# A Fourier filter woven into a feed-forward block: the forward transform over s by three real products per complex one

## The chip, the cores and the metric

The kernel runs on one core of a Trainium2 chip. The metric is the device time of one execution in microseconds (us); the time before is the median of three runs. A profile is one further execution, recorded by the hardware profiler.

## The reference, cut to what matters

```python
def reference(x, w_r, w_i, _, w1, w2):            # x 1 x 2048 x 1024, F = 3584
    xn = layernorm(x)
    X = rfft2(xn, axes=(-2, -1))                  # 2048 x 513, complex
    s = irfft2(X * (w_r + 1j * w_i), (2048, 1024), axes=(-2, -1))
    g = silu(silu(xn @ w1) @ w2)
    return x + s * g
```

One branch is a two-dimensional Fourier filter, the other a feed-forward block; both start from the same normalised rows and meet in the last line. The axis of 2048 rows is called s, the axis of 1024 columns d.

## The kernel before

**The feed-forward block** is the bulk of the work of PE, the matmul engine (TensorE). `mm1` (line 456, tile `pa`) multiplies the rows by w1 in groups of 24 matmuls of 128x512; `mm2` (lines 539 to 541, tile `pb`) multiplies by w2 in seven products of a Strassen-like scheme, in half-groups of 21 matmuls. Between the two the hidden rows go to DRAM as sums and differences (`hd_sum`, `hd_one`, `hd_dif`) and come back as `ht`. Weights for w2 come in 256 KB pieces (`jr`, line 412), and are converted by ACT and DVE (ScalarE and VectorE, tile `w`, lines 251 and 254).

**The filter branch** is cut into generators that are woven between these groups. `ln_gen` normalises; `fd_gen` (lines 798 to 893) is the forward transform over d, four blocks c of 512 rows; `f_gen` (from line 924) is the forward transform over s with the filter and the first part of the inverse; `edge_gen` treats the last column; `i_gen` is the inverse, for the four c in the order 1, 3, 0, 2, with tile `iu` (lines 1204 and 1212) and tile `id` (line 1294), and a butterfly behind each `id` (lines 1305 to 1340).

At its end `fd_gen` makes for each c four results j: `radix4` writes `Ro` (real part in columns 0 to 127, imaginary in 128 to 255 of each of four rows q). `high_r` (ACT) and `low_r` (DVE, line 865) split it into a high and a low f16 half, `Rs`, and a deferred SP instruction stores `Rs` in the DRAM tile `vd{j}` (line 866). When all is stored, `close` (through `switch`) frees the pool of this stage, and `open_f` opens the next one, in the same memory.

`f_gen` works through 16 blocks u = 4q + j. `load_v` brings `vq{u}` (512 KB, two buffers), `load_w` the two filter pieces `wq` (256 KB each, four buffers), `load_k`, issued by ACT, the constants `kq` for each q. `mat(u)` computes the complex product with the constants k = (-sin, cos, sin) on PE, tile `fx`. For each of four c and each of three pairings of high and low halves it issues one matmul of 256 columns with cos (both parts at once) and two of 128 columns with the sines: 36 matmuls, lines 954 to 956. `fx` fills one of the two PSUM buffers with tag `ft`, which `fa`, `fx`, `iu` and `id` share. `copy(u)` (ACT, line 975) copies half of `fx` to SBUF, and two instructions of DVE of 512 elements (`xb` and `xd`, lines 1004 and 1005) add and subtract the halves. Then DVE multiplies by the filter and transforms back, `T`, `yb`, `yd`, `Z`, `zq`.

**What sets the order.** Everything is written out by hand in one program order; each engine takes its instructions in that order and waits on semaphores. After every group of `pa` or half-group of `pb` the function `work` lets the next step of a generator run, as long as a model of DVE's time is not over a model of PE's by more than `LEAD` = 1 us. `meter` keeps both models: an instruction of DVE adds a fixed and a per-element part.

```python
    COST = {"DVE": ("dve", 0.12, 1.05e-3), "PE": ("pe", 0.0, 0.4215e-3)}
...
            clock["dve"] = max(clock["dve"], clock["pe"] - 1.0)
            for _ in range(3):
                if clock["dve"] > clock["pe"] + LEAD or hold[0] or slot(bg) == PAUSE:
                    break
```

`defer(n, fn)` issues fn n such ticks later. Nearly all DMAs are issued by SP (SyncE), strictly in order. SP's DMAs use eight semaphores in turn, `DMAHW0` to `DMAHW7`, and a DMA waits until the one before it on the same semaphore has landed.

Of the kernel before, what the change touches and what calls it, by code (L numbers as in the profile page):

```python
# [43 lines left out]
def make_constants():  # L44
# [16 lines left out]
    k = np.stack([-np.sin(th), np.cos(th), np.sin(th)], 3)  # L61
# [66 lines left out]
def spectral_ffn(ctx, tc, x, w_r, w_i, w1, w2, ca, kc, ci, tw, pm, out):  # L128
# [19 lines left out]
    vd = [dp.tile([128, 4, 4, 2, 256], F16, name=f"vd{j}") for j in range(4)]  # L148
    zd = [dp.tile([128, 4, 2, 1024], F16, name=f"zd{c}") for c in range(4)]
# [62 lines left out]
    COST = {"DVE": ("dve", 0.12, 1.05e-3), "PE": ("pe", 0.0, 0.4215e-3)}  # L212
# [563 lines left out]
    psa, l0 = {}, {}  # L776

# [17 lines left out]
    def fd_gen(c):  # L795
# [3 lines left out]
        def bfly(p):  # L799
            t0 = l0.pop((c, p))  # L800
            tt, stt = nc.vector.tensor_tensor, nc.vector.scalar_tensor_tensor
# [56 lines left out]
        o, sp = {}, {}  # L858

        def high_r(j):  # L860
            sp[j] = ap.tile([128, 4, 2, 256], F16, name=f"Rs{c}_{j}", tag="Rs", bufs=2)
            nc.scalar.activation(sp[j][:, :, 0], o[j], AF.Copy, scale=2.0**-21)
# [55 lines left out]
    def open_f():  # L918
# [3 lines left out]
        B["k"], B["v"], B["w"], B["z"] = {}, {}, {}, {}  # L922

    def f_gen():
# [12 lines left out]

        def load_w(u):
# [8 lines left out]
        def mat(u):  # L947
            q = u // 4
            ps = pt.tile([128, 4, 2, 128], F32, name=f"fx{u}", tag="ft")
            v, k = B["v"].pop(u), B["k"][q]  # L950
            for c in range(4):
                o = ps[:, c].rearrange("m r k -> m (r k)")
                for n, (kh, vh) in enumerate(((0, 0), (0, 1), (1, 0))):
                    nc.tensor.matmul(o, k[:, c, kh, 1], v[:, c, vh], start=(n == 0), stop=False)  # L954
                    nc.tensor.matmul(ps[:, c, 0], k[:, c, kh, 2], v[:, c, vh, 128:256], start=False, stop=False)  # L955
                    nc.tensor.matmul(ps[:, c, 1], k[:, c, kh, 0], v[:, c, vh, 0:128], start=False, stop=(n == 2))
            psx[u] = ps
# [3 lines left out]
        load_v(0)  # L961
        load_w(0)
# [33 lines left out]
        for u in range(16):  # L996
# [3 lines left out]
            ps, cpy = psx.pop(u), cps.pop(u)  # L1000
            pv = ps.rearrange("m c r k -> m c (r k)")
            b = bp.tile([128, 2, 2, 128], F32, name=f"xb{u}", tag="xb", bufs=1)
            d = bp.tile([128, 2, 2, 128], F32, name=f"xd{u}", tag="xd", bufs=1)
            tt(b.rearrange("m c r k -> m c (r k)"), pv[:, 0:2], cpy, op=OP.add)
            tt(d.rearrange("m c r k -> m c (r k)"), pv[:, 0:2], cpy, op=OP.subtract)
# [619 lines left out]
```

## Time and profile before

| | us |
|---|---|
| median of three runs | 1235.48 |
| the runs | 1234.14 to 1237.49 |
| the profiled execution | 1235.84 |
| its span | 1234.1 |
| PE busy | 1220.7 (99%) |
| DVE busy | 999.0 (81%) |
| ACT busy | 467.6 (38%) |
| POOL (GpSimd) busy | 117.3 (10%) |

The span runs from the first to the last recorded instruction; the profiled execution's own time has in addition what lies around it. In rows of a timeline the first number is the start in us from the start of the span, the second the duration; `x3` says that the row holds three instructions; a bracket at the end tells how long the engine was idle before it, and what it waited for. Matmuls are pipelined: they start more closely than their durations say. The granted clock of PE was at its full value in every part of the profile.

### The profile page before, as it was taken

Reading aid. Unit: us, or ns where it says so; the run is one execution under the profiler, and the core shown is the slowest. Engines: PE = TensorE matmul, PEld = TensorE weight load, DVE = VectorE, ACT = ScalarE, POOL = GpSimd, SP = SyncE. Lnnn points to the kernel's source line nnn. Section 1 sums busy time; section 2 is a strip of 40 time slices with the busy share of each in tenths; the row PEclk is TensorE's granted clock in tenths of the full one; section 3 lists DMA queues with packets and bytes.
Section 4 is the critical chain, followed back from the end, with each engine's and each line's share of the span. In section 5 each row is a group of like instructions: output and inputs, shape, how many; then the busy total and the mean of one; then the engine's idle time right before and its main releaser. Section 6 shows DMA issues by size and latency. Waiting matters only on the chain.

```text
span 1234.1 us, 19097 instructions
## 1 busy us (share of the span) xinstructions
PE 1220.7 (99%) x7033; PEld 625.2 (51%) x7033; DVE 999.0 (81%) x1970; ACT 467.6 (38%) x614; POOL 117.3 (10%) x245
## 2 busy tenths in 40 slices
PE   8999999999999999999999999999999999999998
PEld 5545445444544454445545555554455555555545
DVE  7687988899798898896969899985186678798886
ACT  4865344333554565444433222122032222243212
POOL 2330000001000000010001121114111111000000
PEclk9999999999999999999999999999999999999999
DMA  7487476655758898759898999997989999998576
GB/s 253 134 172 187 135 224 201 185 152 161 223 172 237 276 283 242 217 177 279 207 283 224 283 259 198 276 256 246 293 207 278 286 289 331 315 332 325 200 261 260
DMA packets 271102, 293.67 MB, mean 238 GB/s; under 512 B 40096, under 2 KB 198816, under 8 KB 270624
## 3 DMA queue, kind: packets, MB, share of 16 engines
q1 hardware_dynamic: 250992, 233.66, 65.7%
q10 hardware_dynamic: 15984, 51.45, 12.0%
q0 software_dynamic: 4032, 7.34, 3.5%
q8 instruction: 55, 0.90, 0.3%
q14 instruction: 39, 0.32, 0.1%
HBM read 185.95 MB, written 102.25 MB: 234 GB/s over the span
## 4 chain that ended last, share of the span: by engine, by line
PE 75%; DVE 11%; DMA 9%; issue 2%; ACT 1%; SPq 0%; POOL 0%; DVEq 0%; ACTq 0%; POOLq 0%
PE pa L456 45%; PE pb L539 8%; PE pb L541 8%; PE pb L540 8%; DVE Z L1055 2%; DMA wq<-in_A_w_i_dram 2%; DMA sd<-s 2%; PE id L1294 2%; DMA zd<-zq 1%; DMA ht<-hd_sum_d 1%; DVE T L1020 1%; DVE w L254 1%; PE iu L1204 1%; ACT xp L709 1%; PE iu L1212 1%
## 5 line engine op out<-in xcount | busy, mean ns | idle before, releaser
L456 PE MATMUL pa<-xnT,w 128*128 128x512 f16 x2688 | 585.2, 379 | 1.1 <-ACT w L251 0.7
L456 PEld LDWEIGHTS <-w 128*128 128x128 f16 x2688 | 262.2, 98 | 311.6 <-DVE w L254 1.3
L539 PE MATMUL pb<-w,ht 128*128 128x512 f16 (+2 forms) x812 | 300.4, 372 | 0.0
L540 PE MATMUL pb<-w,ht 128*128 128x512 f16 (+2 forms) x812 | 300.4, 372 | 0.0
L541 PE MATMUL pb<-w,ht 128*128 128x512 f16 (+2 forms) x812 | 300.3, 372 | 0.0
L541 PEld LDWEIGHTS <-ht 128*128 128x128 f16 x812 | 79.4, 98 | 91.0
L539 PEld LDWEIGHTS <-ht 128*128 128x128 f16 x812 | 79.5, 98 | 86.7
L540 PEld LDWEIGHTS <-ht 128*128 128x128 f16 x812 | 79.4, 98 | 86.7
L465 ACT ACTIVATE h<-pa,s 128x512 f32<-128x512 f32 x112 | 75.5, 678 | 122.9 <-PE pa L456 111.0
L251 ACT ACTIVATE w<-jr,sc 128x512 f16<-128x512 f32 x98 | 68.1, 713 | 77.8 <-PE pb L541 22.1
L254 DVE SCALAR_TENSOR_TENSOR w<-jr,sc,w 128x512 f16<-128x512 f32 x98 | 71.1, 744 | 2.1 <-ACT w L251 2.1
L254 DVE SCALAR_TENSOR_TENSOR hoone<-h,hs,hoone 128x2048 f16<-128x2048 f32 x28 | 65.6, 2344 | 7.9 <-ACT hoone L251 7.9
L251 ACT ACTIVATE hoone<-h,hs 128x2048 f16<-128x2048 f32 x28 | 56.0, 1998 | 36.5 <-DVE h L499 24.3
L251 ACT ACTIVATE hosum<-hr,hs 128x1536 f16<-128x1536 f32 x28 | 44.1, 1574 | 64.1 <-DVE hr L495 26.8
L981 ACT ACTIVATE zq<-Z,zs 128x1024 f16<-128x1024 f32 x16 | 18.4, 1149 | 103.9 <-DVE Z L1055 57.0
L494 DVE TENSOR_TENSOR hr<-h 128x1024 f32<-128x1024 f32 x28 | 34.2, 1221 | 24.4 <-ACT h L465 24.3
L254 DVE SCALAR_TENSOR_TENSOR hosum<-hr,hs,hosum 128x1536 f16<-128x1536 f32 x28 | 50.7, 1812 | 3.1 <-ACT hosum L251 3.1
L251 ACT ACTIVATE w<-w1r,rs 128x1024 f16<-128x1024 f32 x28 | 31.9, 1144 | 47.0 <-DVE w L254 31.8
L274 DVE TENSOR_REDUCE m<-w1r 128x1 f32<-128x1024 f32 x28 | 33.8, 1210 | 16.1 <-DMA w1r<-in_B_w_dram 16.1
L632 ACT ACTIVATE pl<-pl,c 128x512 f32<-128x512 f32 (+2 forms) x28 | 17.6, 657 | 70.1 <-DVE pl L608 41.6
L954 PE MATMUL fx<-vq,kq 128*128 128x256 f16 x192 | 43.2, 273 | 0.0
L955 PE MATMUL fx<-vq,kq 128*128 128x128 f16 x192 | 42.0, 219 | 0.0
(219 smaller groups left out, 1524.8 us busy)
## 6 DMA issues: line engine op xcount, KB each, us to landing
w1r<-in_B_w_dram SPq DMA_DIRECT2D x28, 512.0 KB, 6.2
hd_sum<-hosum SPq DMA_DIRECT2D x56, 256.0 KB, 2.9
hd_one<-hoone SPq DMA_DIRECT2D x56, 256.0 KB, 3.7
hd_dif<-hoone SPq DMA_DIRECT2D x56, 256.0 KB, 3.2
w2m<-in_B_w_dram SPq DMA_DIRECT2D x28, 512.0 KB, 5.2
ht<-hd_dif ACTq DMA_DIRECT2D x32, 448.0 KB, 6.3
jr<-in_B_w_dram SPq DMA_DIRECT2D x56, 256.0 KB, 6.8
ht<-hd_sum ACTq DMA_DIRECT2D x32, 448.0 KB, 6.4
```

The source lines that it names most:

```text
L251: nc.scalar.activation(hi, raw, AF.Copy, scale=scale)
L254: nc.vector.scalar_tensor_tensor(lo, raw, scale, hi, op0=OP.mult, op1=OP.subtract)
L274: nc.vector.tensor_reduce(m1[:, i:i + 1], raw[i], axis=AX.XY, op=OP.max, apply_absolute_value=True)
L456: nc.tensor.matmul(ps, w[:, wh, d], xt[:, xh, d], start=(n == 0), stop=(n == 23))
L465: nc.scalar.activation(hq[:, 2 * (c % 2) + f % 2], ps, AF.Silu, scale=s1[:, f:f + 1])
L494: tt(sums[:, 0:2], hq[:, 0::2], hq[:, 1::2], op=OP.subtract)
L539: nc.tensor.matmul(ps, hh[:, 0], w[:, 0], start=first, stop=False)
L540: nc.tensor.matmul(ps, hh[:, 0], w[:, 1], start=False, stop=False)
L541: nc.tensor.matmul(ps, hh[:, 1], w[:, 0], start=False, stop=last)
L954: nc.tensor.matmul(o, k[:, c, kh, 1], v[:, c, vh], start=(n == 0), stop=False)
L955: nc.tensor.matmul(ps[:, c, 0], k[:, c, kh, 2], v[:, c, vh, 128:256], start=False, stop=False)
L1055: eng.tensor_tensor(Z[:, ns, pos], x0[:, :, ls], x1[:, :, ls], op=o_)
```

## The change

1. The constants become k = (cos, sin - cos, -sin - cos). A complex product is then three real ones: cos times the sum of both parts (which serves both results), and the two others times one part each.
2. The sum of both parts is a third operand. `fd_gen` adds it on DVE (`total`, 512 elements per partition for each c and j), splits it into high and low halves (`both`, one instruction of ACT, one of DVE) and stores them with two DMAs of 128 KB in new DRAM tiles `vs{j}`. `put` lets these stores go before the tiles that they read are written anew, since `total` and `both` use buffers of `bfly`.
3. `load_s(u)` brings `vs{u}` (256 KB, one buffer), for u+1 one tick after `mat(u)`.
4. `mat(u)` issues 36 matmuls of 128 columns, 18 into each of two PSUM tiles with tag `ft`.
5. `copy(u)` is two instructions of ACT, which copy the common product twice into an SBUF tile; two new instructions of DVE add the two others from PSUM to it. `xb` and `xd` then read SBUF.
6. The model of DVE's time has new numbers.

```diff
-    k = np.stack([-np.sin(th), np.cos(th), np.sin(th)], 3)
+    k = np.stack([np.cos(th), np.sin(th) - np.cos(th), -np.sin(th) - np.cos(th)], 3)
...
+    vs = [dp.tile([128, 4, 4, 2, 128], F16, name=f"vs{j}") for j in range(4)]
...
-    COST = {"DVE": ("dve", 0.12, 1.05e-3), "PE": ("pe", 0.0, 0.4215e-3)}
+    COST = {"DVE": ("dve", 0.09, 1.0417e-3), "PE": ("pe", 0.0, 0.4215e-3)}
...
+    unput = []
+
+    def put():
+        while unput:
+            d = unput[0]
+            deferred.remove(d)
+            d[1]()
...
         def high_r(j):
+            put()
+            both[j] = [ap.tile([128, 4, 128], F16, name=f"vt{c}_{j}_{h}", tag=tag, bufs=1) for h, tag in enumerate(("EE", "EO"))]
+            nc.scalar.activation(both[j][0], total[j], AF.Copy, scale=2.0**-21)
...
             nc.vector.scalar_tensor_tensor(sp[j][:, :, 1], o[j], 2.0**-21, sp[j][:, :, 0], op0=OP.mult, op1=OP.subtract)
+            nc.vector.scalar_tensor_tensor(both[j][1], total[j], 2.0**-21, both[j][0], op0=OP.mult, op1=OP.subtract)
             defer(2, lambda: nc.sync.dma_start(vd[j][:, :, c], sp[j]))
+
+            def sums():
+                unput.remove(d)
+                for h in range(2):
+                    nc.sync.dma_start(vs[j][:, :, c, h], both[j][h])
+
+            d = [2, sums]
+            deferred.append(d)
+            unput.append(d)
...
+            total[j] = ap.tile([128, 4, 128], F32, name=f"vt{c}_{j}", tag="E", bufs=1)
+            nc.vector.tensor_tensor(total[j], o[j][:, :, 0:128], o[j][:, :, 128:256], op=OP.add)
             yield 3.9
...
+        def load_s(u):
+            q, j = u // 4, u % 4
+            B["s"][u] = bp.tile([128, 4, 2, 128], F16, name=f"vs{u}", tag="vs", bufs=1)
+            nc.sync.dma_start(B["s"][u], vs[j][:, q])
...
-            ps = pt.tile([128, 4, 2, 128], F32, name=f"fx{u}", tag="ft")
-            v, k = B["v"].pop(u), B["k"][q]
-            for c in range(4):
-                o = ps[:, c].rearrange("m r k -> m (r k)")
-                for n, (kh, vh) in enumerate(((0, 0), (0, 1), (1, 0))):
-                    nc.tensor.matmul(o, k[:, c, kh, 1], v[:, c, vh], start=(n == 0), stop=False)
-                    nc.tensor.matmul(ps[:, c, 0], k[:, c, kh, 2], v[:, c, vh, 128:256], start=False, stop=False)
-                    nc.tensor.matmul(ps[:, c, 1], k[:, c, kh, 0], v[:, c, vh, 0:128], start=False, stop=(n == 2))
-            psx[u] = ps
+            v, t_, k = B["v"].pop(u), B["s"].pop(u), B["k"][q]
+            for half in range(2):
+                ps = pt.tile([128, 2, 512], F32, name=f"fx{u}_{half}", tag="ft")
+                for i, c in enumerate((half, half + 2)):
+                    for g, src in enumerate((t_[:, c], v[:, c, :, 128:256], v[:, c, :, 0:128])):
+                        for n, (kh, vh) in enumerate(((0, 0), (0, 1), (1, 0))):
+                            nc.tensor.matmul(ps[:, i, 128 * g:128 * g + 128], k[:, c, kh, g], src[:, vh], start=(n == 0), stop=(n == 2))
+                psx[u, half] = ps
+            if u + 1 < 16:
+                defer(1, lambda: load_s(u + 1))
...
-            cps[u] = bp.tile([128, 2, 256], F32, name=f"xc{u}", tag="xc", bufs=1)
-            nc.scalar.activation(cps[u], psx[u].rearrange("m c r k -> m c (r k)")[:, 2:4], AF.Copy)
+            cps[u] = bp.tile([128, 2, 2, 2, 128], F32, name=f"xo{u}", tag="T1", bufs=1)
+            for half in range(2):
+                nc.scalar.activation(cps[u][:, half], psx[u, half][:, :, 0:128].unsqueeze(2).broadcast_to([128, 2, 2, 128]), AF.Copy)
...
+            full = cps.pop(u)
+            for half in range(2):
+                planes = psx.pop((u, half))[:, :, 128:384].rearrange("m i (r k) -> m i r k", r=2)
+                tt(full[:, half], full[:, half], planes, op=OP.add)
+            pv = full.rearrange("m h i r k -> m i h (r k)")
...
-            tt(b.rearrange("m c r k -> m c (r k)"), pv[:, 0:2], cpy, op=OP.add)
-            tt(d.rearrange("m c r k -> m c (r k)"), pv[:, 0:2], cpy, op=OP.subtract)
+            tt(b.rearrange("m c r k -> m c (r k)"), pv[:, 0], pv[:, 1], op=OP.add)
+            tt(d.rearrange("m c r k -> m c (r k)"), pv[:, 0], pv[:, 1], op=OP.subtract)
```

The change also moves instructions. In the queue of SP near the start of `f_gen` the load `vs1` is new. These are the changed program's rows from the load of `wq1` on (tiles with their buffer numbers; `<-` names what is read; a bracket names the semaphores that are waited for):

```order
L971 DMA wq1_1_5600<-in_A_w_i_dram 128x4x128 [waits DMAHW0_49]
L489 DMA hd_one_0_0_98<-hoone_0_12_0_5585 512x1x256 [waits DMAHW1_49,DVE_49]
L489 DMA hd_dif_1_0_90<-hoone_0_12_0_5585 512x1x256 [waits DMAHW2_49]
L489 DMA hd_dif_0_0_92<-hoone_0_12_0_5585 512x1x256 [waits DMAHW3_49]
L489 DMA hd_one_3_0_96<-hoone_0_12_0_5585 512x1x256 [waits DMAHW4_49]
L413 DMA jr5_5635<-ws0_5_147 128x512 [waits DMAHW5_49]
L413 DMA jr6_5668<-ws0_6_148 128x512 [waits DMAHW6_49,DVE_49]
L959 DMA vq2_5713<-vd2_77 128x2048 [waits DMAHW7_49,PE_49]
L413 DMA jr7_5731<-ws0_7_149 128x512 [waits DMAHW0_49,DVE_49,Activation_49]
L965 DMA vs1_5765<-vs1_80 128x1024 [waits DMAHW1_49]
```

`vs1` stands behind vq2 and jr7, and waits for the store eight places ahead of it. On PE its reader `fx1` stands one group of 24 matmuls (tile `pa2_23`) behind `fx0`. Without the rows that only repeat, the changed program has there:

```order
L984 MATMUL fx0_0_5672<-vs0_5524,kq0_5471 128x128 [waits DMAHW6_49]
L984 MATMUL fx0_1_5691<-vs0_5524,kq0_5471 128x128
L457 MATMUL pa2_23_5735<-xnT2_675,w1_23_4599 128x512 [waits Activation_49]
L984 LDWEIGHTS kq0_5471 [waits DMAHW1_49]
L984 MATMUL fx1_0_5771<-vs1_5765,kq0_5471 128x128 [waits DVE_49]
L984 MATMUL fx1_0_5771<-vq1_5596,kq0_5471 128x128 [waits DMAHW6_49]
L984 MATMUL fx1_1_5790<-vs1_5765,kq0_5471 128x128 [waits DVE_49]
```

In the program before, `fx0` stands behind `pa2_23` and one group (`pa3_22`) lies between it and `fx1`; the block has moved one group to the front, and `fx1` waits for DVE, which frees the buffers of `fx0`, as well as for its loads.

The third place is the inverse on PE, block c = 1; the second number of `id` is the number p of the butterfly. The rows that matter, of the program before:

```order
L1294 MATMUL id1_0_9162<-cis_8509,us1_0_8837 128x130 [waits Activation_49]
L1294 MATMUL id1_1_9187<-cis_8509,us1_0_8837 128x130 [waits PE_49]
L539 LDWEIGHTS ht3_4_1_8972 [waits DMAHW6_49]
L539 MATMUL pb3_4_9131<-w2_3_1_8381,ht3_4_1_8972 128x512
L1294 LDWEIGHTS us1_0_8837 [waits DVE_49,PE_49]
L1294 MATMUL id1_2_9260<-cis_8509,us1_0_8837 128x130 [waits Activation_49]
```

Two blocks `id` are followed by 21 matmuls of `pb`, and these by the third block. The same place in the changed program:

```order
L1329 MATMUL id1_0_9534<-cis_8901,us1_0_9248 128x130 [waits Activation_49]
L1329 MATMUL id1_1_9559<-cis_8901,us1_0_9248 128x130 [waits PE_49]
L1329 LDWEIGHTS us1_0_9248 [waits DVE_49,PE_49]
L1329 MATMUL id1_2_9605<-cis_8901,us1_0_9248 128x130 [waits Activation_49]
L540 LDWEIGHTS ht3_7_0_9382 [waits DMAHW3_49]
L540 MATMUL pb3_7_9655<-w2_3_0_8097,ht3_7_0_9382 128x512
```

The 24 matmuls of each `id` follow each other; the waits of the third block are for ACT and DVE, which empty the PSUM buffer of the first. The 21 matmuls of `pb` that lay between the second block and the third now lie behind the third.

More of the change, by code (lines that the diff above doesn't have):

```diff
@@ L857, in fd_gen @@
             yield 0
-        o, sp = {}, {}
+        o, sp, total, both = {}, {}, {}, {}
         def high_r(j):
+            put()
+            both[j] = [ap.tile([128, 4, 128], F16, name=f"vt{c}_{j}_{h}", tag=tag, bufs=1) for h, tag in enumerate(("EE", "EO"))]
+            nc.scalar.activation(both[j][0], total[j], AF.Copy, scale=2.0**-21)
             sp[j] = ap.tile([128, 4, 2, 256], F16, name=f"Rs{c}_{j}", tag="Rs", bufs=2)
@@ L921, in open_f @@
         B["p"] = B["es"].enter_context(tc.tile_pool(name="flt", bufs=1, side="right"))
-        B["k"], B["v"], B["w"], B["z"] = {}, {}, {}, {}
+        B["k"], B["v"], B["s"], B["w"], B["z"] = {}, {}, {}, {}, {}
     def f_gen():
@@ L961, in f_gen @@
         load_v(0)
+        load_s(0)
         load_w(0)
@@ L999, in f_gen @@
                 high_z(u - 1)
-            ps, cpy = psx.pop(u), cps.pop(u)
-            pv = ps.rearrange("m c r k -> m c (r k)")
+            full = cps.pop(u)
[3 more added lines that the diff above has]
+            pv = full.rearrange("m h i r k -> m i h (r k)")
             b = bp.tile([128, 2, 2, 128], F32, name=f"xb{u}", tag="xb", bufs=1)
             d = bp.tile([128, 2, 2, 128], F32, name=f"xd{u}", tag="xd", bufs=1)
-            tt(b.rearrange("m c r k -> m c (r k)"), pv[:, 0:2], cpy, op=OP.add)
-            tt(d.rearrange("m c r k -> m c (r k)"), pv[:, 0:2], cpy, op=OP.subtract)
+            tt(b.rearrange("m c r k -> m c (r k)"), pv[:, 0], pv[:, 1], op=OP.add)
+            tt(d.rearrange("m c r k -> m c (r k)"), pv[:, 0], pv[:, 1], op=OP.subtract)
             X = bp.tile([128, 8, 128], F32, name=f"X{u}", tag="X", bufs=2)
```

## The prediction

> **What bounds the kernel now.** The profiled execution took 1235.84 us, 1234.1 us of it the span, so 1.74 us lie around it. The page's first and fourth parts come first.
>
> ```profile
> PE 1220.7 (99%) x7033; PEld 625.2 (51%) x7033; DVE 999.0 (81%) x1970; ACT 467.6 (38%) x614; POOL 117.3 (10%) x245
> ...
> PE 75%; DVE 11%; DMA 9%; issue 2%; ACT 1%; SPq 0%; POOL 0%; DVEq 0%; ACTq 0%; POOLq 0%
> ```
>
> PE, the matmul engine, is busy for 99% of the span. Every microsecond of matmul that goes is a microsecond won, and every new wait of PE is one lost: there is no idle time to take it up. The chain still gives 20% to DVE and DMA, so elsewhere than in the matmuls something is nearly late. The waits of PE show how little is late today:
>
> ```profile
> PE tp L718 <- ACT x L709: 3.0, 3, 2.0
> PE iu L1212 <- DVE ub L1221: 1.7, 1, 1.7
> ```
>
> These are the two largest (total, times, longest); PE never waits for the forward transform over s (tile `fx`) or its loads. The prediction asks whether that stays so.
>
> **The columns of PE.** One block u of `fx` is 36 matmuls; the timeline of PE has the first one:
>
> ```profile
> 576.77 0.27 PE L954 MATMUL fx<-vq,kq 128*128 128x256 f16 x1
> 576.88 0.22 PE L955 MATMUL fx<-vq,kq 128*128 128x128 f16 x1
> 576.93 0.22 PE L956 MATMUL fx<-vq,kq 128*128 128x128 f16 x1
> 576.99 0.27 PE L954 MATMUL fx<-vq,kq 128*128 128x256 f16 x1
> ...
> 579.42 2.75 PE L456 MATMUL pa<-xnT,w 128*128 128x512 f16 x12
> ```
>
> Matmuls overlap, so a start counts to the next start, not the duration: 256 columns cost 0.11 us, 128 columns about 0.055, the block 579.42 - 576.77 = 2.65. Afterwards it is 36 matmuls of 128 columns. Such a run stands in the chain of waits for the inverse:
>
> ```profile
> 895.68 2.68 PE iu L1204 x48
> ```
>
> 2.68 / 48 = 0.0558 us each, so the block becomes 36 x 0.0558 = 2.01 us, and 16 blocks save 16 x 0.64 = **10.3 us**. A rival reading is that each weight load (there is one per matmul) sets the spacing:
>
> ```profile
> L954 PEld LDWEIGHTS <-kq 128*128 128x128 f16 x192 | 18.8, 98 | 1.9
> ```
>
> At 98 ns a block would be 3.53 us, 0.88 longer, and the change would cost 14.1 us here instead. The 48 `iu` matmuls have a load each and run at 56 ns, so I give it 3 in 100. The Trainium skill, "TensorE: Matmul & The Clock Gate", section "Back-to-back issue gap", speaks against the change in the same way: a stream of load and matmul pairs of 128 columns settles near 81 ns, because both operations set the spacing. By that figure a block would be an estimated 2.92 us and the change would lose 4 us where I count a gain; the row of `iu` disagrees, and the measurement decides.
>
> **DVE and ACT.** Per u DVE gains two adds of 512 elements, per (c, j) of the transform over d one add and one f16 difference of 512. The spacing of such adds, and the length of one u today:
>
> ```profile
> 717.54 0.68 DVE L1004 TENSOR_TENSOR xb<-fx,xc 128x512 f32<-128x512 f32 x1
> 718.14 0.68 DVE L1005 TENSOR_TENSOR xd<-fx,xc 128x512 f32<-128x512 f32 x1
> ...
> 728.81 0.68 DVE L1004 TENSOR_TENSOR xb<-fx,xc 128x512 f32<-128x512 f32 x1
> ...
> 734.81 1.41 DVE L254 SCALAR_TENSOR_TENSOR w<-jr,sc,w 128x512 f16<-128x512 f32 x2
> ```
>
> An add is 0.60 us and an f16 difference of 512 some 0.66, so a u of 11.27 us of DVE becomes 12.5, and each (c, j) has 1.26 more: 16 x (1.2 + 1.26) = 39 us, 999 to 1038 of the span. It costs nothing by sums: with the pacing's numbers the changed program puts 63 matmuls of 512 columns (13.6 us) and a block (2.0) between one `fx` and the next, 15.6 us, and DVE has some 2 us of weight conversions and accumulations beside the 12.5 (two take 1.41 in the last row). That cover is thin, though. With five matmuls fewer between, 1.1 us, DVE would be the bound.
>
> Until now `fx` of u+1 had its second PSUM buffer. A u now holds both, so `fx` of u+1 waits for the two adds of u, which stand 9.1 us of PE work (42 matmuls of 5.18 / 24 = 0.216, a row further down) ahead of it in the program. DVE goes from one u to the next without a pause in the rows above, so it can well run as far as that behind the program; a wait here and a wait for the load of u+1, below, end at the same matmul, and I count them together. ACT gets one more copy and one f16 half of 512 elements at some 0.7 us each (the evacuation of 560.07 below has that size), 32 x 0.7 = 22 us in all, at 38% busy: nothing.
>
> **The end of the forward transform over d.** The pool is closed when its last stores have landed, and ACT issues the load of the next constants behind that:
>
> ```profile
> 552.26 1.06 ACT L862 ACTIVATE Rs<-Ro 128x1024 f16<-128x1024 f32 x1 [7.90 <-DVE Ro L241]
> 559.64 0.39 ACTq L929 DMA_DIRECT2D kq<-in_kc_dram  x1
> 560.07 0.69 ACT L465 ACTIVATE h<-pa,s 128x512 f32<-128x512 f32 x1 [6.75 <-DMA vd<-Rs]
> ```
>
> A group of `pa` on PE is 24 matmuls in 5.18 us:
>
> ```profile
> 579.58 5.18 PE pa L456 x24
> ```
>
> ACT sits still for 6.75 us there. Its evacuation from 560.07 to 560.76 frees the PSUM buffer of the group that starts three groups ahead of 576.77, at 576.77 - 15.5 = 561.2: half a microsecond of slack. Now four stores of 128 KB (two `vs` pairs) join the queue ahead of it, and the stretch has thirteen issues instead of ten. At SP's spacing of about 0.6 us per issue (570.44 below) that is 1.8 us, plus up to 2 for landing; less 0.5 of slack I take a PE wait of **1.8 us** (0 to 3.5).
>
> **The first load of sums.** In the changed order `fx1` follows `fx0` by one group of 24 matmuls (5.2 us), and `vs1`, which has one buffer, is issued behind vq1, the two wq1, four stores, jr5, jr6, vq2 and jr7. SP and the transfers today:
>
> ```profile
> 570.44 0.52 SPq L488 DMA_DIRECT2D hd_one<-hoone  x1
> ...
> 576.11 0.45 SPq L935 DMA_DIRECT2D vq<-vd  x1
> ...
> 577.68 5.08 SPq L412 DMA_DIRECT2D jr<-ws  x3
> 582.86 1.94 SPq L935 DMA_DIRECT2D vq<-vd  x1
> ```
>
> ```profile
> vq<-vd SPq DMA_DIRECT2D x1, 512.0 KB, 9.7
> jr<-ws SPq DMA_DIRECT2D x1, 256.0 KB, 10.2
> ```
>
> ```profile
> 560.00:576.00 16.00, 16.00 (x76) 7.25 (x75) 12.68 (x12) 9.93 (x12) 0.00 (x0) 1.00 0.99 320
> 576.00:600.00 24.00, 24.00 (x161) 13.48 (x160) 17.55 (x31) 10.74 (x15) 2.07 (x5) 1.00 1.00 234
> ```
>
> (The last two columns are DMA share and GB/s; the pair above is issues and us to landing for 582 to 584.) The DMA engines are full. Today vq2, behind 3.0 MB from 570.44 on, is issued at 582.86 and lands 9.7 later, 592.6. Up to `vs1` the new queue carries the same: 1.0 (stores) + 0.75 (three jr) + 1.0 (two vq) + 0.5 (wq1) + 0.25 = 3.5 MB. So it lands near 592.6. `fx0` would stand one group earlier, 576.77 - 5.2 = 571.6; with 2.0 and 5.2 `fx1` is wanted at 578.8, or 580.6 with the 1.8 above. PE waits **12 us**: at the least 1.5 (3.5 MB at 320 GB/s from 570.44 end at 582), at the most 16, if the 3.5 us of the stage's close push the queue too.
>
> **The other loads of sums.** From u=4 on `vs` of u+1 stands on SP right behind the two wq of u+1, 9.1 us of PE work ahead of its use.
>
> ```profile
> jr<-ws SPq DMA_DIRECT2D x17, 256.0 KB, 5.7
> ...
> wq<-in_A_w_i_dram SPq DMA_DIRECT2D x4, 256.0 KB, 10.3
> ```
>
> ```profile
> 755.57 15.34 DMA wq<-in_A_w_i_dram
> ```
>
> ```profile
> 750.00:800.00 50.00, 50.00 (x305) 26.63 (x303) 49.86 (x95) 10.35 (x14) 7.64 (x17) 1.00 0.96 232
> ```
>
> The queue's head takes 5.7 us to land at 560 to 640, a second wq 10.3, one later 15.3 (the chain), and the engines are 0.96 busy. By the lowest a `vs` is in time: 0. By 10.3 plus 0.7 of issue a load is 1.9 late; at 11 u's that is 21. A wait isn't paid in full each time, since the queue drains while PE stands: I take half, **10 us** (0 to 20).
>
> **The inverse.** In the changed program the matmuls of `id2` stand right behind `id1`, and wait for the adds on `id0`'s result; today 21 matmuls lie between.
>
> ```profile
> 937.14 3.21 PE L1294 MATMUL id<-cis,us 128*128 128x130 f16 x48
> ```
>
> ```profile
> 940.29 0.67 DVE L1308 TENSOR_TENSOR sk<-id,sc 128x504 f32<-128x504 f32 x1
> ```
>
> `id1` is over at 937.14 + 3.05 = 940.19 (the next start), the add at 940.96: about 0.7 us for each of four c, **2.6 us** (0 if ACT is early, 5 if DVE is behind). The pacing's new numbers bring this; the other moves I cost at nothing, since the work moved keeps PE's 0.216 us matmuls beside it.
>
> **The sum:** 1235.84 - 10.3 + 1.8 + 12 + 10 + 2.6 = 1251.9, **1252 us**. The profiled execution is 0.36 us above the median 1235.48, inside the runs' 1234.14 to 1237.49, so nothing is corrected.
>
> **Rivals.** (a) The loads are in time, because today's order of issue is late only where the queue can afford it: then -10.3 + 1.8 + 2.6 is left, 1230. For it speaks that PE waits for no load today; it decides if `vs1` lands before 581 and each later `vs` within 9 us. The full DMA shares speak against. Chance 10 in 100. (b) Only `fx1` waits, by 8 us, the rest not: 1238, within 0.3%; 8 in 100. (c) Each u waits for DVE and load both, at the upper ends: 1235.84 - 10.3 + 3.5 + 16 + 20 + 3 = 1268; 14 in 100. (d) Weight loads set the spacing: 14.1 + 10.3 = 24.4 more than the sum, 1276; 3 in 100. The forecast itself, the sum with its waits, has 65.
>
> **Range and chances.** 1237 to 1268 takes in the forecast, most of (b) and (c) and leaves out (a) and (d). A measurement can tell about 0.3% from no change, 1231.8 to 1239.2: faster 0.10, within 0.08, slower 0.82.
>
> **What would show it.** An `fx` block of 2.0 us and starts 0.055 apart show the gain; 2.9 or 3.5 show the weight load. A wait of PE on `fx` for DMA of `vs`, some 12 us near 580 and several of 1 to 5 behind it, shows the loads; waits on `fx` for DVE show the PSUM buffers. Waits on `id` for DVE of 0.7, four times, show the inverse, a longer idle of ACT before the evacuation at 560 the close. If PE's waits stay under 12 us in all, the prediction is wrong and (a) is right.

## The result, and the profile after

The changed kernel takes 1302.89 us (median of six runs, 1295.02 to 1307.97), the kernel before 1236.99 beside it: a ratio of 1.0534, 95% interval 1.051 to 1.0557. It is 66 us slower, where 16 were forecast. The profiled execution took 1304.98 us, 1303.1 of it the span, 69.0 more than before. These are the rows of its page that answer to those shown of before, and the row of the granted clock over 40 slices of the span, which was all 9 before:

```profile
PE 1233.7 (95%) x7033; PEld 630.3 (48%) x7033; DVE 1041.4 (80%) x2034; ACT 482.3 (37%) x646; POOL 118.3 (9%) x245
...
PEclk9999999999999999988999998899999999899999
```

PE is busy 13 us longer although it has 10 us less to do, and it stands for 69 us instead of 13. The waits of PE name whom it stood for (total, times, longest; the smaller rows are left out):

```profile
PE fx L984 <- DMA vs<-vs: 30.6, 7, 11.7
PE pa L457 <- ACT h L466: 9.9, 3, 7.0
PE iu L1247 <- DVE sk L1343: 5.5, 1, 5.5
PE iu L1247 <- DVE ub L1256: 3.4, 2, 2.5
PE id L1329 <- DVE sk L1343: 3.0, 4, 0.8
PE fx L984 <- ACT w L252: 2.8, 1, 2.8
PE fa L790 <- ACT L L800: 2.5, 1, 2.5
```

No row of `fx` stood in this list before. The timeline of PE at the longest wait, the first load of sums, shows the gain and both losses in one place:

```profile
608.34 0.50 PE L984 MATMUL fx<-vs,kq 128*128 128x128 f16 x3 [11.66 <-DMA vs<-vs]
608.63 0.85 PE L984 MATMUL fx<-vq,kq 128*128 128x128 f16 x6
609.27 0.53 PE L984 MATMUL fx<-vs,kq 128*128 128x128 f16 x3
609.59 0.85 PE L984 MATMUL fx<-vq,kq 128*128 128x128 f16 x6
610.23 0.53 PE L984 MATMUL fx<-vs,kq 128*128 128x128 f16 x3
610.55 0.77 PE L984 MATMUL fx<-vq,kq 128*128 128x128 f16 x6
611.16 0.33 PE L984 MATMUL fx<-vs,kq 128*128 128x128 f16 x3
611.33 0.50 PE L984 MATMUL fx<-vq,kq 128*128 128x128 f16 x6
611.66 0.59 PE L457 MATMUL pa<-xnT,w 128*128 128x512 f16 x2
```

PE stands for 11.66 us. Then six matmuls take 609.27 - 608.63 = 0.64 us, 0.107 each; the last six take 611.66 - 611.33 = 0.33, 0.055 each. From 608.34 to 611.1, some 2.7 us, every matmul runs at half speed. That is the second loss, and the forecast had no term for it.

To count it I went through all matmuls of the trace and compared the distance from each start to the next with the usual one of its size (0.216 us for 512 columns, 0.056 for 128). A distance more than 0.3 us over the usual is a stop; what is left over is slow clock.

| us | before | after | difference | forecast |
|---|---|---|---|---|
| usual distances of all matmuls | 1223.8 | 1213.5 | -10.3 | -10.3 |
| stops | 8.4 | 68.2 | +59.8 | +26.4 |
| slow clock (difference) | | | +19.5 | 0 |
| span | 1234.1 | 1303.1 | +69.0 | +16.1 |

### The profile page after: what moved, and what is told of

Its sections match the earlier page's. It is cut to its first block, busy times and chain, and to the rows that moved or that the text cites. A ratio compares the mean times of both kernels' runs of the same rounds, so it can differ in the third digit from the quotient of the medians.

```text
span 1303.1 us, 19231 instructions
## 1 busy us (share of the span) xinstructions
PE 1233.7 (95%) x7033; PEld 630.3 (48%) x7033; DVE 1041.4 (80%) x2034; ACT 482.3 (37%) x646; POOL 118.3 (9%) x245
## 5 line engine op out<-in xcount | busy, mean ns | idle before, releaser
L252 ACT ACTIVATE hoone<-h,hs 128x2048 f16<-128x2048 f32 x28 | 55.9, 1996 | 50.0 <-DVE h L500 26.4
L984 PEld LDWEIGHTS <-kq 128*128 128x128 f16 x576 | 42.1, 115 | 39.2 <-DMA vs<-vs 34.1
L1007 ACT ACTIVATE xo<-fx 128x512 f32<-128x512 f32 x32 | 18.8, 597 | 110.0 <-PE fx L984 100.2
L984 PE MATMUL fx<-vs,kq 128*128 128x128 f16 x192 | 25.2, 249 | 33.4 <-DMA vs<-vs 30.6
L1035 DVE TENSOR_TENSOR xo<-xo,fx 128x512 f32<-128x512 f32 x32 | 21.2, 682 | 26.3 <-ACT xo L1007 26.2
```

The source lines that it names most:

```text
L252: nc.scalar.activation(hi, raw, AF.Copy, scale=scale)
L984: nc.tensor.matmul(ps[:, i, 128 * g:128 * g + 128], k[:, c, kh, g], src[:, vh], start=(n == 0), stop=(n == 2))
L1007: nc.scalar.activation(cps[u][:, half], psx[u, half][:, :, 0:128].unsqueeze(2).broadcast_to([128, 2, 2, 128]), AF.Copy)
L1035: tt(full[:, half], full[:, half], planes, op=OP.add)
```

## Experiments

**E1, the numbers of the pacing model alone.**

```diff
-    COST = {"DVE": ("dve", 0.12, 1.05e-3), "PE": ("pe", 0.0, 0.4215e-3)}
+    COST = {"DVE": ("dve", 0.09, 1.0417e-3), "PE": ("pe", 0.0, 0.4215e-3)}
```

> The kernel before with the new numbers of the pacing model alone; nothing else of the change. Theory A (the pacing's numbers bring the waits of the inverse): the waits of PE on id for DVE appear as in the changed kernel, about 0.8 us four times, with or without those on iu: 1238 to 1252 us. Rival B (those waits come from the extra work of DVE in the transforms, which the model of time only passes on): no new wait on id or iu, 1235 to 1237 us.

Measured: 1250.10 us, ratio 1.0113 (1.0087 to 1.0139). Theory A holds. Its waits of PE:

```profile
PE eps L1085 <- POOL edge L1078: 3.7, 1, 3.7
PE id L1294 <- DVE sk L1308: 3.0, 4, 0.8
```

The wait on `id` is the one forecast. The one on the edge column (`eps`) was not, and 4.4 us of slow clock follow it. So a table of two numbers costs 14 us, without a product or a transfer changed.

**E2, two buffers for the loads of sums, two blocks ahead** (and five `jr` for six, to make room).

```diff
-            B["s"][u] = bp.tile([128, 4, 2, 128], F16, name=f"vs{u}", tag="vs", bufs=1)
+            B["s"][u] = bp.tile([128, 4, 2, 128], F16, name=f"vs{u}", tag="vs", bufs=2)
...
-            if u + 1 < 16:
-                defer(1, lambda: load_s(u + 1))
...
                 load_v(u + 3)
+                load_s(u + 3)
```

> The changed kernel with two buffers for the loads of sums, each issued right behind the load vq of the same block, two blocks ahead; to make room the jr pieces have five buffers for six. Theory A (the order and the single buffer make the loads late): the 33 us of waits on fx go, and with them the slow clock behind them, some 10 us: 1303 - 43 = about 1260 us, mean clock 0.985 or more. Rival B (the DMA engines cannot carry the 8.4 MB more): the waits move to other loads (jr, wq, ht) and the time stays above 1285 us.

Measured: 1270.08 us, ratio 1.0272 (1.0241 to 1.0302), clock 0.988. No wait of `fx` on a load is left, and none moved to `jr` or `wq`; the largest waits are now these:

```profile
PE pa L457 <- ACT h L466: 9.6, 3, 6.8
PE iu L1248 <- DVE sk L1344: 4.5, 1, 4.5
PE id L1330 <- DVE sk L1344: 3.8, 4, 1.5
PE fx L984 <- DVE xo L1035: 3.3, 2, 2.6
```

Theory A holds for the mechanism, with 33 us won instead of 43. The bytes were not the limit: the same 8.4 MB travel here.

**E3, no sums at all** (stores, loads and additions of the sums are taken out).

```diff
-                    for g, src in enumerate((t_[:, c], v[:, c, :, 128:256], v[:, c, :, 0:128])):
+                    for g, src in enumerate((v[:, c, :, 0:128], v[:, c, :, 128:256], v[:, c, :, 0:128])):
```

> The changed kernel without the sums of both parts: they are neither added, split, stored nor loaded, and the matmuls read the real part in their place (so the output is not the reference's). What stays are the 36 matmuls of 128 columns, the two PSUM tiles for a block, the two extra adds and copies and the new pacing numbers. Theory A (the price lies in the transfers of the sums and their waits): about 1303 - 33 (fx) - 7 (end of the transform over d) - 13 (slow clock behind them) = 1250 us; what is above 1225 lies in waits on id and iu. Rival B (matmuls of 128 columns or the shared PSUM buffers give no gain): waits on fx for DVE appear, or the spacing is above 0.06 us, and the time stays above 1270 us.

Measured: 1246.65 us, ratio 1.0075 (1.0046 to 1.0105). Forming and moving the sums thus costs 1302.9 - 1246.7 = 56 us. The usual distances add up to 1213.5 us, so the columns do save 10.3; but PE still stands in the inverse:

```profile
PE iu L1229 <- DVE sk L1325: 7.0, 1, 7.0
PE iu L1229 <- DVE ub L1238: 3.4, 2, 2.5
PE id L1311 <- DVE sk L1325: 3.0, 4, 0.8
```

Theory A holds. `fx` waits for nothing here, so the PSUM buffers that a block now fills alone are not the problem in this run; in E2 the block does wait 3.3 us for the adds of the one before.

**E4, six stops put into the kernel before.** Between two small matmuls ACT copies a tile once and then 2, 6, 9, 12, 20 or 40 times more, and PE has to wait for that.

```diff
+            nc.tensor.matmul(ps[:, 0:128], idle[:, 0:128], idle[:, 0:128], start=True, stop=True)
+            nc.scalar.activation(stall, ps[:, 0:128], AF.Copy)
+            for _ in range(n):
+                nc.scalar.activation(stall, stall, AF.Copy)
+            nc.tensor.matmul(ps[:, 128:256], stall, idle[:, 0:128], start=True, stop=True)
```

> The kernel before with six stops of PE of growing length in the stretch of pb, each a chain of copies on ACT between two small matmuls. It measures the clock behind a stop alone. Theory A (each stop of PE over about 2.5 us is followed by matmuls at half speed, and shorter ones are not): behind stops under 2.2 us the spacing of 512 columns stays 0.216 us; behind those over 2.6 us some 6 to 12 matmuls stand 0.43 us apart, 1.3 to 2.9 us lost each. Rival B (the clock falls with the mix of small matmuls or with DMA load, not with the stop): no half-speed matmuls behind any stop.

Measured: one run, 1277.11 us. The matmuls behind five of the stops on PE:

```profile
839.86 0.23 PE L1476 MATMUL gap<-ones,stall 128*128 128x128 f16 x1 [1.05 <-ACT stall L1475]
...
853.60 0.23 PE L1476 MATMUL gap<-ones,stall 128*128 128x128 f16 x1 [2.48 <-ACT stall L1475]
...
866.45 0.29 PE L1476 MATMUL gap<-ones,stall 128*128 128x128 f16 x1 [3.50 <-ACT stall L1475]
...
881.99 0.29 PE L1476 MATMUL gap<-ones,stall 128*128 128x128 f16 x1 [4.52 <-ACT stall L1475]
...
901.01 0.29 PE L1476 MATMUL gap<-ones,stall 128*128 128x128 f16 x1 [7.25 <-ACT stall L1475]
```

The durations alone tell it: 0.23 us behind the two short stops, 0.29 behind the others. No slow matmul follows the stops of 1.05 and 2.48 us; 9, 13, 8 and 14 matmuls 0.43 us apart follow the other four (the last stood 14.1), 1.7, 2.4, 1.5 and 2.7 us lost. The run took 41.5 us more than the kernel before beside it (1235.66); the stops add up to 32.9 and the slow matmuls to 8.3. Theory A holds, with two of the counts above its 12, and the loss does not grow with the stop. The Trainium skill, "TensorE: Matmul & The Clock Gate", section "What's actually happening", says that the clock gate goes to half after an idle window of about 3.4 us and back after a busy one, and that the window runs freely; the trace agrees with the half and with a loss that varies from stop to stop. It does not bear out 3.4 us as the least stop: in the last section 17 of 27 distances of 2.5 to 3.4 us were followed by half speed, and the measurement decides.

**E5, the split sums of even and odd j in different buffers.**

```diff
-enumerate(("EE", "EO"))
+enumerate((("EE", "EO"), ("DS", "P"))[j % 2])
```

> The changed kernel, in which the split sums of odd j use two other buffers than those of even j, so that ACT's half of j need not wait for the stores of j-1. Theory A (the 7 us stop of PE at the end of the transform over d comes from ACT's wait of 10.6 us for the store before): the stop falls to 3 us or less and the slow clock behind it goes: 1295 to 1299 us. Rival B (the last stores' landing alone sets that stop): it stays 6 to 7 us, 1301 to 1304 us.

Measured: 1293.82 us (1290.03 to 1299.08), ratio 1.0459 (1.0421 to 1.0496). At the end of the transform over d ACT stood twice in the changed kernel, for the store of j = 2 and for the last stores:

```profile
568.96 0.63 ACT L872 ACTIVATE vt<-vt 128x512 f16<-128x512 f32 x1 [10.60 <-DMA vs<-vt]
569.50 1.04 ACT L874 ACTIVATE Rs<-Ro 128x1024 f16<-128x1024 f32 x1
576.44 0.39 ACTq L953 DMA_DIRECT2D kq<-in_kc_dram  x1
576.88 0.69 ACT L466 ACTIVATE h<-pa,s 128x512 f32<-128x512 f32 x1 [6.34 <-DMA vs<-vt]
```

In E5 it no longer waits for the store of j = 2 (0.92 us for DVE instead), but 15.5 us for the last stores:

```profile
552.04 0.63 ACT L872 ACTIVATE vt<-vt 128x512 f16<-128x512 f32 x1 [0.92 <-DVE vt L904]
552.57 1.04 ACT L874 ACTIVATE Rs<-Ro 128x1024 f16<-128x1024 f32 x1
568.69 0.39 ACTq L953 DMA_DIRECT2D kq<-in_kc_dram  x1
569.13 0.69 ACT L466 ACTIVATE h<-pa,s 128x512 f32<-128x512 f32 x1 [15.51 <-DMA vs<-vt]
```

PE's stop stays at 6.5 us. Theory A falls: the last stores in SP's queue set it, though ACT stands ready for them for 15.5 us and not 6.3 (why they come late stands below, under the close). The 9 us won lie in shorter stops earlier in that stage (the wait of `fa` for ACT is gone) and in the scatter of these runs.

**E6, the loads of sums issued by ACT right behind the block before.**

```diff
-            nc.sync.dma_start(B["s"][u], vs[j][:, q])
+            nc.scalar.dma_start(B["s"][u], vs[j][:, q])
...
-                defer(1, lambda: load_s(u + 1))
+                load_s(u + 1)
```

> The changed kernel with one buffer as it is, but each load of sums issued by ACT right behind the matmuls of the block before, not by SP one tick later behind the queue. Theory A (what makes the loads late is SP's queue and its waits for transfers eight places back): most of the 33 us of waits on fx go, the first one (12 us) falls to 3 to 6; 1265 to 1275 us. Rival B (the DMA engines themselves are full, whoever issues): the waits on fx stay above 20 us, 1290 us or more.

Measured: 1269.81 us, ratio 1.0267 (1.0244 to 1.029).

```profile
PE fx L984 <- DMA vs<-vs: 6.2, 3, 3.3
```

Theory A's times hold, down to the first wait of 3.3, and rival B falls. One buffer is enough if the load is issued early. The edit takes away SP's queue and the tick of delay at once, so it does not tell how much of the lateness each of them made.

**E7, the new numbers on the kernel before, with three forced breaks.**

```diff
-            yield 3.4 if p else 0.3
+            yield PAUSE if p == 1 else 3.4 if p else 0.3
```

(and two `PAUSE` ahead of the matmuls of the edge column)

> The kernel before with the new numbers of the pacing model, as in the first experiment, and three forced breaks in the weave: one between the second and the third id of the inverse, two ahead of the matmuls of the edge column. Theory A (the new numbers cost 14 us because several steps of a generator come in one go, so PE stands for DVE and POOL, and the clock falls behind the longest stop): the waits on id (3.0) and on the edge (3.7, with 4.4 of slow clock behind) go, 1250 - 11 = 1237 to 1240 us. Rival B (the cost lies in the changed order as a whole): other waits come in their place, above 1245 us.

Measured: 1239.59 us, ratio 1.0015 (1.0000 to 1.0029). Theory A holds: the waits on `id` and on the edge are gone, and the clock is whole again; two short waits of E1 grow, from 1.6 to 3.3 us for a load of `ht` and from 1.8 to 3.2 for ACT, and 1.3 us are left beside the kernel before (1238.26). So most of the 14 us comes from letting several steps go at once in a few places, not from the changed order as a whole.

**E8, E10, E11, mended versions of the change.** E8 has E2's buffers, E5's and the breaks of E7 with three more in the inverse's third block. E10 and E11 have E6's issue, the first load early into memory of a tile that is not yet in use, E5's buffers, E9's issue of `kq` and the breaks of E7; E11 has one break more. The lines are of E10 and E11.

```diff
+            B["s"][u] = bp.tile([128, 4, 2, 128], F16, name=f"vs{u}", tag="zq" if u == 1 else "vs", bufs=1)
+            (nc.scalar if u > 1 else nc.sync).dma_start(B["s"][u], vs[j][:, q])
```

> The changed kernel with two buffers for the loads of sums (five for jr), the alternating buffers of the split sums, and forced breaks in the weave: those on id and the edge as in the run on the kernel before, and three in the inverse's third block, whose iu waited for DVE. Theory A (the gain of 10.3 us on PE is there, and every loss is a stop that can be taken away): two buffers alone gave 1270; less the end of the transform over d (7 + 2), id (3), edge (3.1 + 3.8) and iu (7 + 4) gives 1240 us, below it if the stops of 2 us in the transform over d go as well, and then faster than the kernel before. Rival B (the extra DVE and DMA work keeps some engine late wherever it is put): 1250 us or more.

> The changed kernel with its six jr buffers and these mendings: loads of sums issued by ACT right behind the block before; the first one early, into memory that is not yet in use; the alternating buffers of the split sums; the first kq by SP; the breaks on id and the edge. Theory A (each loss is a stop that can be taken away): from the 1270 of the run with ACT as issuer less fx1 (3.5 + 2.8), the end of the transform over d (7.2 + 2.8), the stops within it (2.6 + 1.6) and id (3.0): 1246 us, of which 13 lie in the iu of the third block. Rival B (stops move elsewhere, as they did in the run with five jr buffers): 1255 us or more.

> The same with one break more, between the first and the second iu of the inverse's third block. Theory A (that iu stands for the butterfly before it, 4.7 to 7 us, and a group of matmuls in between covers it): 13 us less 3 for the later waits that stay: 1236 us. Rival B (the later place brings DVE or the accumulation behind it late, since the branch then ends too close to the end): no gain or a loss against the run without it.

Measured: 1262.88 (ratio 1.0198, 1.0173 to 1.0222), 1256.18 (1.0135, 1.0094 to 1.0176) and 1259.24 us (1.0152, 1.0114 to 1.0191). Most of the mended stops are gone. E8 keeps the one at the close (6.5 us, as in E5), and `fx` still waits for loads of sums, 4.8 us in E10 and 8.3 in E11. New stops stand in the inverse, up to 10.2 us (E8). Ahead of them DVE stands for rows of the feed-forward block that were stored because the filter branch was not there yet, and now come back (`gd`); the first row is of E8, the second of E10:

```profile
1066.60 0.75 DVE L624 SCALAR_TENSOR_TENSOR fs<-s,s_sc,fs 128x512 f32<-128x512 f32 x1 [9.27 <-DMA fs<-gd]
1054.43 0.75 DVE L624 SCALAR_TENSOR_TENSOR fs<-s,s_sc,fs 128x512 f32<-128x512 f32 x1 [8.43 <-DMA fs<-gd]
```

Rival B holds in E8 and E11 and, at 1256 against its 1255, narrowly in E10.

**E9, the first load of `kq` issued by SP.**

```diff
-            nc.scalar.dma_start(t_, kf[q])
+            (nc.scalar if q else nc.sync).dma_start(t_, kf[q])
```

> The changed kernel, in which SP and not ACT issues the first load of the constants kq, so that ACT no longer waits for the last stores of the transform over d before it evacuates the next group. Theory A (PE's stop of 7 us there is ACT standing in line for the freed pool): the stop falls below 1 us, and with it 1.4 to 2 us of slow clock: 1303 - 8.5 = 1294 us. Rival B (the stop is due to the stores themselves: SP or another engine waits for the same landing): it stays above 5 us, 1300 us or more.

Measured: 1300.23 us, ratio 1.0491 (1.0464 to 1.0517).

```profile
PE fx L984 <- DMA vs<-vs: 39.2, 9, 13.5
PE pa L457 <- ACT h L466: 4.6, 4, 2.0
```

At that place the stop of 7.0 falls to two of 0.6 and 1.3 (the 2.0 stands elsewhere), so it was ACT in line behind the load: theory A holds for the stop, not for its time of 1294. The time stays near 1300, because `fx` then waits 8.6 us more. Of these 4.7 stand at the first two blocks, where PE comes to the same late loads earlier, and 3.8 at the seventh, for which this run shows no reason.

**E12, the sums formed by POOL in the core's own memory**, from E3 with numbers between the old and the new.

```diff
+                g.tensor_tensor(t, v[:, c, 0, 0:128], v[:, c, 0, 128:256], op=OP.add)
+                g.tensor_copy(s_[:, c, 0], t)
+                g.tensor_tensor(t, t, s_[:, c, 0], op=OP.subtract)
+                g.tensor_tensor(t, t, v[:, c, 1, 0:128], op=OP.add)
+                g.tensor_tensor(s_[:, c, 1], t, v[:, c, 1, 128:256], op=OP.add)
```

> The three products without any transfer of sums: nothing is added or stored in the transform over d; instead POOL forms the high and low half of the sum in the memory of the core from the loaded vq, twenty instructions of 128 elements for each block, right behind the block before. The numbers of the pacing model lie between the old and the new ones (0.105, 1.045e-3). Theory A (the price of the change lies in the transfers of the sums and in stops that the pacing brings): from the 1247 of the run without sums some 5 to 12 us of stops in the inverse go, if POOL has a sum ready in the 13 us between two blocks: 1235 to 1243 us. Rival B (POOL is too slow, or slows DVE): waits on fx for POOL, 1255 us or more.

Measured: 1308.66 us, ratio 1.0581 (1.0556 to 1.0605). Rival B holds:

```profile
PE fx L976 <- DVE xo L1027: 19.6, 9, 3.2
...
PE fx L976 <- POOL vs L957: 7.3, 5, 1.8
```

An instruction of 128 elements takes POOL 0.61 to 0.70 us, twenty of them 13 us per block, and the products with the filter on DVE take 1.37 us beside it instead of 1.22.

**E13, E14, E15, numbers between** (0.105 and 1.045e-3; E15 0.1), on E3 and on the mended kernel without breaks.

```diff
-    COST = {"DVE": ("dve", 0.09, 1.0417e-3), "PE": ("pe", 0.0, 0.4215e-3)}
+    COST = {"DVE": ("dve", 0.105, 1.045e-3), "PE": ("pe", 0.0, 0.4215e-3)}
```

> The run without sums (not added, split, stored or loaded, the real part read in their place, so the output is not the reference's) with numbers of the pacing model between the old and the new (0.105, 1.045e-3). Theory A (of the 1247 of that run the 20 us above 1225 are stops that the new numbers bring, as they bring 14 to the kernel before): the stops on iu and id shrink to under 6 us, 1228 to 1236 us, so the gain on PE is there to be had. Rival B (those stops come from the two added PSUM reads and the shared PSUM tiles): 1243 us or more.

> The mended kernel (loads of sums by ACT, the first one early, alternating buffers of the split sums, first kq by SP), without forced breaks and with the numbers between (0.105, 1.045e-3). Theory A (with the transfers mended the rest is pacing): from the 1256 of the mended run, 14 us of stops in the inverse less 4 that stay, 1242 to 1248 us. Rival B (with the work of DVE for the sums the branch ends too late, whatever the numbers): stops of 5 us and more stay in the inverse, 1252 us or more.

> The same with (0.1, 1.045e-3), nearer to the new numbers: the branch ends one to three half-groups earlier. Theory A: 1242 to 1250 us, near the run beside it. Rival B: 1252 us or more, as there.

Measured: 1256.59 (ratio 1.0158, 1.0121 to 1.0195), 1287.70 (1.0418, 1.0394 to 1.0441) and 1273.91 us (1.0305, 1.0281 to 1.0328). Theory A falls in all three. In E14 and E15 rival B holds: PE stands 11.0 and 11.5 us on `id` and 10.6 and 9.2 on `pb`. In E13 its cause is not seen, since `fx` waits for nothing there. With these numbers the branch ends later: in E13 the kernel needs 13.1 us behind the start of its last matmul, 4.9 before and in the changed kernel. On its way DVE waits (E13):

```profile
1049.73 0.75 DVE L624 SCALAR_TENSOR_TENSOR fs<-s,s_sc,fs 128x512 f32<-128x512 f32 x1 [10.26 <-DMA fs<-gd]
```

This wait parts all the runs cleanly. Where the last matmul of `id` starts 31 to 41 us before the end of the span (E8 and E10 to E15) DVE waits 9 to 12 us for `gd`; where it starts 50 us or more before it (all others) it never does. So forced breaks and the numbers between seem to go wrong in the same way: the branch comes too late for these rows of the feed-forward block. No run was faster than the kernel before.

## Why the prediction was wrong

**The sign, the place of the first stop and the gain were right.** The columns of PE saved 10.3 us. The weight loads do not set the spacing: 0.055 us behind the slow stretch, not 0.081 as the Trainium skill, "TensorE: Matmul & The Clock Gate", section "Back-to-back issue gap", has it, nor 0.098. `vs1` was to cost 12 us and cost 11.7, partly by luck. The forecast let the load be issued 9.5 us behind the start of `fx0` (582.86 against 571.6 + 1.8) and land 9.7 later; it was issued 12.8 us behind (602.10 against 589.33) and the wait ended 6.2 later. `id` was to cost 2.6 and cost 3.0; the forecast's own rows, 940.96 - 940.19 four times, give 3.1. Which of the rows were sized wrong, stops against stops:

| stop, us | forecast | measured |
|---|---|---|
| close of the transform over d | 1.8 | 7.0 (longest of `pa` for ACT) |
| `vs1` | 12 | 11.7 |
| later blocks of `fx` | 10 | 21.7 (30.6 + 2.8 - 11.7) |
| `id` | 2.6 | 3.0 |
| `iu` for DVE | 0 | 7.2 (5.5 + 3.4 less 1.7 before) |
| slow clock behind stops | 0 | 19.5 |

The stops named add up to 50.6 of the 59.8 us; the others are short ones of `pa` and `fa`, none over 2.5 us, and what the two ways of counting differ by.

**The step that failed first: a stop was priced at its own length.** The forecast added waits at their length and had no term for the clock, which was at its full value throughout the profile of before. That profile has no stop over 2.3 us, so it could not show what follows a long one. E4 shows it by itself: each longer stop costs 1.5 to 2.7 us more. With 19.5 us this is the largest term that was missing.

**The discount on the later loads was wrong, and so was what it was taken from.** The forecast worked out 1.9 us for each of 11 blocks, 21 in all, and took half, "since the queue drains while PE stands". The measured 21.7 is near the full sum, but by luck: seven blocks wait, 0.2 to 8.5 us, and the others not at all. (2.8 of it is put down to ACT by the page; in E9 the same block waits for its load.) Most of the eleven loads are issued 2.5 to 3.7 us behind the start of the last matmul of the block before, whether PE had stood or not, so a stop gives the next load no lead. Two are issued 9 us behind it, and their blocks wait 2.9 and 4.0. The worst was issued in time and landed late; here it is, issued by SP behind a pair of `wq`, with the start of its reader on PE:

```profile
809.60 0.51 SPq L971 DMA_DIRECT2D wq<-in_A_w_i_dram  x1
810.20 1.19 SPq L965 DMA_DIRECT2D vs<-vs  x1
```

```profile
830.38 0.50 PE L984 MATMUL fx<-vs,kq 128*128 128x128 f16 x3 [8.53 <-DMA vs<-vs]
```

E2 takes these waits away and E6 most of them, by issuing earlier, with the same bytes. That also corrects a reading: the full DMA share was taken to mean that the engines were the limit.

**The close was undersized, and not for the reason that was priced.** The forecast counted SP's issues: "that is 1.8 us, plus up to 2 for landing; less 0.5 of slack". But the stretch from SP's first `hd_sum` to the issue of `kq` hardly grew, from 13.6 us (546.09 to 559.64) to 14.2 (562.24 to 576.44). It starts later. These are its first rows, before and changed:

```profile
546.09 1.21 SPq L488 DMA_DIRECT2D hd_sum<-hosum  x2
```

```profile
562.24 1.21 SPq L489 DMA_DIRECT2D hd_sum<-hosum  x2
```

The group of `pa` whose evacuation stands behind the load of `kq` (the 96th in both programs) is over on PE at 545.9 and 554.6. So the stretch starts 0.2 us behind it before and 7.6 in the changed kernel. SP waits there for DVE's `hosum`, which ends at 546.03 and 562.17, and DVE has become full in this stage; the rows, before and changed, give the length, then PE, its weight loads, DVE and ACT busy:

```profile
500.00:520.00 20.00, 20.00 (x94) 9.11 (x93) 14.90 (x32) 9.12 (x13) 0.00 (x0) 1.00 0.88 261
```

```profile
510.00:530.00 20.00, 20.00 (x94) 9.05 (x93) 19.89 (x39) 10.46 (x14) 0.00 (x0) 1.00 0.83 230
```

"It costs nothing by sums" was worked out for the blocks of `fx` alone; for the transform over d, which has half of the 39 us added to DVE, the forecast made no such sum. 7.4 us of later start and 0.6 of longer way, less the 0.5 of slack, make 7.5 of the 7.0 measured. E5 and E9 show the last link: ACT stands behind the landing of the last stores with PE's evacuation in its hand. In E3, without the sums, `kq` is issued at 545.1 and PE does not stop there.

**"The other moves I cost at nothing" was the fourth error.** E1 shows a stop of 3.7 us on the edge column that the new numbers bring on their own, with 4.4 of slow clock; in the changed kernel PE does not stop there. Its 7.2 us more on `iu` are the part that counts: DVE waits for a load of stored rows, and the buffer that `iu` needs is freed behind that.

```profile
1116.68 0.75 DVE L624 SCALAR_TENSOR_TENSOR pl<-fs,s_sc,pl 128x512 f32<-128x512 f32 x1 [8.30 <-DMA fs<-sd]
```

E3, without the sums, has the same wait of DVE (8.1) and the same stop (7.0), and E2, E5, E6 and E9 have the stop too; the kernel before, E1 and E7 have neither. So it does not come from the transfers. It goes with the place that the weave gives the inverse: in all six runs that have it the last `id` starts 59.5 us before the end of the span. What in the change sets that place wasn't tried by itself.

What stays open is whether any weave of this program turns the 10.3 us into time. Nine runs of the changed kernel took stops away (E2, E5, E6, E8 to E11, E14, E15); the best of them won 47 of the 66 us, and new stops stood in the inverse.

## What to carry to other kernels

Where the bounding engine is 99% busy, price a new wait at its length and, where it is over about 2.5 us, a slow clock behind it (here mostly 1.3 to 2.9 us), and look in a profile for stops long enough to show one before taking the clock as given. A load that is issued just ahead of its use behind a busy queue is late whenever that queue or the transfers ahead of it are slow, here for eight of sixteen blocks: issue it where its data are ready, not where its buffer is named. Read an engine's load in the stage where work is added: DVE was 80% busy over the span and full in the transform over d. A table of costs that sets the order of work is part of the change: try it alone, since here it costs 14 us by itself.

## What the runs showed of the hardware

Over the 17 profiles, from 30 us on, distances from one matmul's start to the next under 2.1 us were followed by matmuls at half speed once in 163 times, those of 2.1 to 2.5 us in 2 of 12, those of 2.5 to 3.4 in 17 of 27, those of 3.4 to 4 in 7 of 8 and those over 4 us in all 44; most lost 1.3 to 2.9 us. So there is no sharp threshold, and two profiles of much the same program can differ by some us for that alone: the same stop of `fa`, 2.5 us for ACT, cost 1.6 us more in the changed kernel and nothing in E2.

A high DMA share is no measure of the rate. In the changed kernel from 808 to 831 us, 40 slices:

```profile
DMA  8579995489999979979999899997987898999998
GB/s 100 144 254 394 374 318 127 132 281 381 357 260 79 36 34 33 45 41 50 55 62 110 119 103 94 55 56 55 67 66 112 150 224 235 263 373 391 411 408 347
```

The engines are busy for 0.7 to 0.9 of most slices, yet for eight slices in the middle (4.6 us) they move 33 to 62 GB/s, and at the end of the stretch about 400. The `vs` load of 810.20 above fell into that stretch and took 20.1 us to land. The packets tell which transfers hold the engines there. From 815 to 824 us SP's queue moves 744 packets in 0.38 MB, 512 bytes each, and they take 92.6% of the engines' time (packets, MB, share):

```profile
q1 hardware_dynamic: 744, 0.38, 92.6%
```

From 808 to 830 us 1024 packets of that size were moved, as many as the two `wq` loads ahead of the `vs` load have rows of 512 bytes. They took 169 ns each on average; those of the nine other pairs between 683 and 868 us took 32 to 96. Why these two were so slow is open.
